# Attention: the row sums of two ticks of a pair are inverted together, in the later of the two ticks

## The chip, the cores and the metric

The kernel runs on one core of one Trainium2 chip. The metric is the device time of one execution in microseconds (us). The core has five engines with a queue of instructions each, which they work off in order: TensorE (PE in the profile, its weight loads PEld), VectorE (DVE), ScalarE (ACT), GpSimd (POOL) and SyncE (SP), which issues most of the transfers. An engine waits on semaphores that the others raise.

## The reference, cut to what matters

Three parts follow one another: an attention, a mixture of experts and a gated layer. The change lies in the attention.

```python
# q, k, v: (4, 8, 576, 64) = batch, heads, sequence, head width
scores = scale * np.matmul(q, k.transpose(0, 1, 3, 2))
mask = block_i >= block_j                  # blocks of 64 positions
scores = np.where(mask, scores, -1000000000.0)
scores = scores - np.max(scores, axis=-1, keepdims=True)
attn = np.exp(scores)
attn = attn / (np.sum(attn, axis=-1, keepdims=True) + 1e-09)
return np.matmul(attn, v).astype(np.float32)
```

Its output goes through eight experts of width 1024, weighted by a router that is normalised by rows and columns eight times, and then through a gated layer of width 1536.

## The kernel before

The attention works on 16 pairs of heads (two heads side by side on the 128 partitions). A pair's 576 query rows are nine chunks of 64, and chunk c needs the keys up to its own block, 64 (c+1) of them. A pair is cut into eight ticks u = 0 to 7 (`TICKS`): u=0 holds chunks 0 and 1, u=1 chunks 2 and 3, u=2 to u=5 hold chunks 4 to 7 one by one, and u=6 and u=7 are the two halves of chunk 8. One loop runs over all ticks of all pairs, and the work of a tick u is spread over later ticks:

- in its own tick `scores` (PE, lines 931 and 942, tile s) and `maxima` (DVE: the row maxima, line 954, and the bias of the exponential, line 963);
- one tick later `exps` (ACT, line 971: the exponential into the tile e of its chunk, and the row sums into tile sum);
- two ticks later `normalise`: DVE adds 1e-9 to the sums (line 990, for u=7 line 986) and inverts them (line 991, tile r), and POOL multiplies each chunk's e by its column of r (line 996). For u=6 it does nothing, since chunk 8 has its whole sum only with u=7;
- four ticks later `transposes`: PE turns the multiplied e (lines 1019 for u=0 and u=1, 1028 for the others, tile t), and ACT copies t to tile a (lines 1022 and 1029), which frees t;
- `values` (PE, line 1046, tile x) multiplies with v, and `take` (ACT, line 1061, tile xf) evacuates it.

The program's order is written out by hand: within a tick stand first the scores, then the transposes of four ticks ago, the additions and splits for the experts that are pending (lines 1079, 1088, 188, 190, 193), `normalise` of two ticks ago and the maxima, then the exponentials of the tick before. Between these parts the loop draws, at a fixed rate, pieces of the first two experts' matmuls (lines 537 and 600 on PE, with their evacuations and splits at 554 to 574, 754 and 758 on ACT and DVE), of the splitting of weights (178, 182, 303, 375), and the scaling of the next pairs' q and k (880, 895, 899, and PE's line 110, which spreads a maximum over the partitions). The tile t has one buffer, s three, x one.

The later parts, the experts from line 1293 on and the gated layer, start their own loops when the attention is over.

Of the kernel before, what the change touches and what calls it, by code (L numbers as in the profile page):

```python
# [30 lines left out]
def attention_moe_glu_kernel(  # L31
# [764 lines left out]
    TICKS = [((0, 0, CB), (1, 0, 2 * CB)), ((2, 0, 3 * CB), (3, 0, 4 * CB))]  # L796
    TICKS += [((c, 0, (c + 1) * CB),) for c in range(4, 8)]
    TICKS += [((8, 0, 288),), ((8, 288, 576),)]
    NTK = len(TICKS)
# [5 lines left out]
    def attention(actx):  # L805
# [172 lines left out]
                    )  # L978

        def normalise(p, u):  # L980
            if u == NTK - 2:
                return
            g = st[p]
            cs = slice(TICKS[u][0][0], TICKS[u][-1][0] + 1)
            if u == NTK - 1:
                nc.vector.tensor_scalar(
                    g["r"][:, cs], g["sum"][:, cs], g["sum"][:, NC : NC + 1], 1e-9, op0=ALU.add, op1=ALU.add
                )
            else:
                nc.vector.tensor_scalar_add(g["r"][:, cs], g["sum"][:, cs], 1e-9)  # L990
            nc.vector.reciprocal(g["r"][:, cs], g["r"][:, cs])  # L991
            for c in range(cs.start, cs.stop):
                n = (c + 1) * CB
                ne = 'PPPPPPPPP'[c]
                if ne == 'P':
                    nc.gpsimd.tensor_scalar(  # L996
                        et[c][:, :n], et[c][:, :n], g["r"][:, c : c + 1], 1.0, op0=ALU.mult, op1=ALU.mult
                    )
                elif ne == 'D':
                    nc.vector.tensor_scalar_mul(et[c][:, :n], et[c][:, :n], g["r"][:, c : c + 1])  # L1000
                else:
                    nc.scalar.activation(et[c][:, :n], et[c][:, :n], AF.Copy, scale=g["r"][:, c : c + 1])
# [157 lines left out]
        for tk in range(tot + NTK):  # L1160
            p, u = divmod(tk, NTK)
# [12 lines left out]
            if on(tk - 2):  # L1174
                normalise(*divmod(tk - 2, NTK))
# [578 lines left out]
```

## Time and profile before

| | us |
|---|---|
| median of three runs | 2089.74 (2084.0 to 2094.1) |
| span of the profiled execution | 2083.4 |
| attention in the profiled execution | about 10 to 372 |
| TensorE busy in the span | 1949.0 (94%) |
| VectorE busy in the span | 1620.1 (78%) |
| ScalarE busy | 1379.9 (66%) |
| GpSimd busy | 612.8 (29%) |

The profile is one execution; its span runs from the first to the last instruction, and its own time with what lies around the span is not told apart from the three above. The span is 0.6 us under the fastest of the three runs and 6.3 under the median. Busy shares are means over all stages; only those of the attention's own stretches say something of this change.

### The profile page before, as it was taken

What the parts mean: (1) busy time and instruction counts of PE and PEld (TensorE: products, weight loads), DVE (VectorE), ACT (ScalarE), POOL (GpSimd) and SP (SyncE); (2) the same over time, 40 slices, a digit from 0 to 9 for tenths busy, and PEclk for the clock granted to TensorE, in tenths of its full rate; (3) what the DMA queues carried; (4) which work ended last, traced back from release to release, by engine and by line L of the source; (5) the groups of instructions that cost most, each with busy time, mean ns of one, the idle gap of its engine ahead of it and who ended that gap; (6) DMA issues with size and microseconds to landing.
All of it is one profiled execution on the core that took longest, in us unless ns stands there. A gap on an engine that the chain in (4) does not pass through costs nothing.

```text
span 2083.4 us, 47251 instructions
## 1 busy us (share of the span) xinstructions
PE 1949.0 (94%) x18378; PEld 1672.9 (80%) x18378; DVE 1620.1 (78%) x3455; ACT 1379.9 (66%) x2940; POOL 612.8 (29%) x873
## 2 busy tenths in 40 slices
PE   6789899799999999999999999999999988999998
PEld 3457676698888888888888888888888877988887
DVE  7887765668787887978878788888887877666666
ACT  5665766348777777878777777777776566544442
POOL 4534444102333333333332333333332123000000
PEclk9889999999999999999999999999999999999999
DMA  5433331306687866878668786777877100301112
GB/s 155 112 96 105 84 105 49 122 22 122 120 172 155 172 136 125 178 150 171 132 132 179 149 178 134 153 157 144 180 148 168 37 11 1 87 21 37 47 42 52
DMA packets 168721, 236.41 MB, mean 113 GB/s; under 512 B 16432, under 2 KB 85680, under 8 KB 168496
## 3 DMA queue, kind: packets, MB, share of 16 engines
q0 software_dynamic: 66560, 107.37, 30.8%
q1 hardware_dynamic: 101936, 126.01, 19.9%
q8 instruction: 144, 2.36, 0.5%
q14 instruction: 81, 0.66, 0.1%
HBM read 90.98 MB, written 24.38 MB: 55 GB/s over the span
## 4 chain that ended last, share of the span: by engine, by line
PE 55%; DVE 15%; ACT 5%; DMA 3%; issue 3%; SPq 0%; POOL 0%; ACTq 0%; DVEq 0%
PE abc_m_b L537 11%; PE m_o_b L645 11%; PE m_o_ac L645 8%; PE abc_m_c L537 5%; PE abc_m_a L537 3%; PE abc_v_b L537 3%; PE abc_g_b L537 3%; PE m_go_b L645 3%; PE m_go_ac L645 2%; DVE m_t L704 2%; DVE m_h L193 2%; DMA wr<-in_w_dram 2%; PE abc_v_c L537 1%; DVE w L182 1%; PE abc_g_c L537 1%
## 5 line engine op out<-in xcount | busy, mean ns | idle before, releaser
L537 PEld LDWEIGHTS <-w 128*128 128x128 f16 x6720 | 609.8, 98 | 110.9 <-issue 45.7
L645 PEld LDWEIGHTS <-m_h 128*128 128x128 f16 x5292 | 514.0, 98 | 69.0 <-issue 10.5
L537 PE MATMUL abc_m_b<-xs,w 128*128 128x256 f16 (+1 forms) x3840 | 476.6, 264 | 31.9 <-DVE m_t L559 29.4
L1443 POOL DMA_DIRECT2D acc<-ev x351 | 305.4, 895 | 581.3 <-ACT ev L1447 367.4
L645 PE MATMUL m_o_b<-w,m_h 128*128 128x256 f16 x3024 | 403.5, 273 | 7.9 <-ACT ev L1447 7.7
L645 PE MATMUL m_o_ac<-w,m_h 128*128 128x256 f16 x2268 | 309.4, 273 | 0.4 <-ACT ev L1447 0.4
L537 PE MATMUL abc_m_c<-xs,w 128*128 128x256 f16 (+1 forms) x1920 | 230.7, 263 | 2.2 <-DVE m_h L758 1.6
L1447 ACT ACTIVATE ev<-m_o_b,pe 128x256 f32<-128x256 f32 x351 | 161.7, 476 | 64.0 <-PE m_o_b L645 52.8
L1447 ACT ACTIVATE ev<-m_o_ac,pe 128x256 f32<-128x256 f32 (+1 forms) x234 | 135.7, 580 | 47.8 <-PE m_o_ac L645 46.4
L178 ACT ACTIVATE w<-wr,ws 128x512 f16<-128x512 f32 x210 | 150.5, 723 | 12.7 <-DVE ws L163 10.3
L182 DVE SCALAR_TENSOR_TENSOR w<-wr,ws,w 128x512 f16<-128x512 f32 x210 | 155.5, 747 | 1.4 <-ACT w L178 1.4
L1431 POOL DMA_DIRECT2D acc<-ev_s x65 | 73.6, 1132 | 259.1 <-ACT ev_s L1427 259.1
L683 ACT CAST m_h<-m_t 128x512 f16<-128x512 f32 (+1 forms) x210 | 121.8, 580 | 41.2 <-DVE m_t L704 40.3
L676 ACT ACTIVATE m_h<-m_t 128x512 f16<-128x512 f32 (+1 forms) x210 | 121.8, 582 | 35.8 <-DVE m_t L574 24.9
L193 DVE TENSOR_TENSOR m_h<-m_t,m_h 128x512 f16<-128x512 f32 (+1 forms) x210 | 133.1, 635 | 8.7 <-ACT m_h L683 8.4
L680 DVE SCALAR_TENSOR_TENSOR m_h<-m_t,m_h 128x512 f16<-128x512 f32 (+1 forms) x210 | 132.2, 635 | 5.8 <-ACT m_h L676 5.6
L537 PEld LDWEIGHTS <-gg_w 128*128 128x128 f16 x1260 | 113.5, 98 | 22.2 <-issue 10.7
L996 POOL TENSOR_SCALAR e<-e,r 128x64 f32<-128x64 f32 (+2 forms) x144 | 78.1, 548 | 166.8 <-DVE r L991 111.9
L645 PEld LDWEIGHTS <-g_h 128*128 128x128 f16 x1134 | 111.0, 99 | 18.9 <-issue 5.4
L537 PEld LDWEIGHTS <-gv_w 128*128 128x128 f16 x1260 | 113.6, 98 | 13.2 <-issue 1.7
L537 PE MATMUL abc_m_a<-xs,w 128*128 128x256 f16 (+1 forms) x960 | 117.5, 262 | 0.0
L375 DVE TENSOR_REDUCE wmx<-wr 128x1 f32<-128x512 f32 x128 | 85.7, 679 | 15.0 <-DMA wr<-in_w_dram 14.9
(298 smaller groups left out, 3364.0 us busy)
## 6 DMA issues: line engine op xcount, KB each, us to landing
acc<-ev POOLq DMA_DIRECT2D x351, 256.0 KB, 4.3
wr<-in_w_dram SPq DMA_DIRECT2D x128, 256.0 KB, 4.8
acc<-ev_s POOLq DMA_DIRECT2D x52, 256.0 KB, 4.3
st<-hl SPq DMA_DIRECT2D x48, 144.0 KB, 3.6
raw_g<-in_w_gate_dram SPq DMA_DIRECT2D x12, 512.0 KB, 5.5
raw_v<-in_w_val_dram SPq DMA_DIRECT2D x12, 512.0 KB, 4.5
raw_o<-in_w_out_dram SPq DMA_DIRECT2D x12, 512.0 KB, 5.0
scr_g<-gg SPq DMA_DIRECT2D x21, 256.0 KB, 2.9
```

Source lines behind the costliest of these rows:

```text
L178: nc.scalar.activation(hi, src, AF.Copy, scale=s)
L182: nc.vector.scalar_tensor_tensor(lo, src, s, hi, op0=ALU.mult, op1=ALU.subtract)
L193: nc.vector.tensor_sub(lo, src, hi)
L375: nc.vector.tensor_reduce(g["mx"][:, k : k + 1], g["b"][k // 2][k % 2], axis=AX.XY, op=ALU.max, apply_absolute_value=True)
L537: nc.tensor.matmul(ps[:, f], W[o][:, sh, k, f * P : (f + 1) * P], xs[:, o, mh, k, c0 : c0 + n], start=x not in begun, stop=True, skip_grou ...
L645: nc.tensor.matmul(ps, h[o][:, sh, k, ii * P : (ii + 1) * P], W[o][:, mh, k], start=o in (X11, X12) and k == 0 and j == 0, stop=True, skip ...
L676: nc.scalar.activation(hi, src, AF.Relu)
L680: nc.vector.scalar_tensor_tensor(lo, src, 0.0, hi, op0=ALU.max, op1=ALU.subtract)
L683: nc.scalar.copy(hi, src)
L996: nc.gpsimd.tensor_scalar(et[c][:, :n], et[c][:, :n], g["r"][:, c : c + 1], 1.0, op0=ALU.mult, op1=ALU.mult)
L1443: nc.gpsimd.dma_start(acc[:, x], e, accum_op=ALU.add)
L1447: nc.scalar.activation(e[:, cols], ps, AF.Copy, scale=p)
```

## The change

`normalise` does nothing any more for u = 0, 2, 4 and 6, and for u = 1, 3 and 5 it takes the chunks of the tick before along with its own: DVE adds and inverts four columns at u=1 and two at u=3 and u=5, and POOL then multiplies all their chunks one after the other. u=7 is left as it was, and so are all other functions.

```diff
         def normalise(p, u):
-            if u == NTK - 2:
+            if u < NTK - 1 and u % 2 == 0:
                 return
             g = st[p]
-            cs = slice(TICKS[u][0][0], TICKS[u][-1][0] + 1)
+            cs = slice(TICKS[u - (u < NTK - 1)][0][0], TICKS[u][-1][0] + 1)
             if u == NTK - 1:
```

VectorE's queue in pair 9, before, from the maxima of u=1 (s_1) to those of u=4 (s_4); r_2807 is the pair's tile of inverses:

```order
496 L954 TENSOR_REDUCE negm_2804<-s_1_2853 128x1 x2
498 L990 TENSOR_SCALAR r_2807<-sum_2806 128x2
499 L991 RECIPROCAL r_2807<-r_2807 128x2
500 L954 TENSOR_REDUCE negm_2804<-s_2_2888 128x1
503 L758 SCALAR_TENSOR_TENSOR m_1_h_2915<-m_1_t_2768,m_1_h_2915 128x512
505 L843 TENSOR_REDUCE vmx_2579<-vs_1_2800 128x1
506 L990 TENSOR_SCALAR r_2807<-sum_2806 128x2
507 L991 RECIPROCAL r_2807<-r_2807 128x2
508 L954 TENSOR_REDUCE negm_2804<-s_3_2927 128x1
512 L990 TENSOR_SCALAR r_2807<-sum_2806 128x1
513 L991 RECIPROCAL r_2807<-r_2807 128x1
514 L954 TENSOR_REDUCE negm_2804<-s_4_2962 128x1
```

The same place of VectorE's queue in the changed kernel, where the pair's inverses are r_2753:

```order
442 L954 TENSOR_REDUCE negm_2750<-s_1_2799 128x1 x2
444 L954 TENSOR_REDUCE negm_2750<-s_2_2834 128x1
447 L758 SCALAR_TENSOR_TENSOR m_1_h_2857<-m_1_t_2713,m_1_h_2857 128x512
449 L843 TENSOR_REDUCE vmx_2527<-vs_1_2746 128x1
450 L990 TENSOR_SCALAR r_2753<-sum_2752 128x4
451 L991 RECIPROCAL r_2753<-r_2753 128x4
452 L954 TENSOR_REDUCE negm_2750<-s_3_2869 128x1
456 L954 TENSOR_REDUCE negm_2750<-s_4_2906 128x1
```

The two instructions for u=0 ahead of s_2 are gone, those ahead of s_3 now hold four columns, and those of u=2 ahead of s_4 have moved on to the place of u=3. Over the whole program VectorE has 96 instructions fewer, six in each of 16 pairs.

GpSimd's queue in pair 9, before, from the multiplication of chunk 4 (e_132, tick u=2) to that of chunk 7 (e_137, u=5); the rows at 1088, 188 and 1079 are pending additions and splits for the experts:

```order
222 L996 TENSOR_SCALAR e_132<-e_132,r_2807 128x320
223 L1088 TENSOR_TENSOR s_8_1_2999<-xf_8_1_2997 128x160
224 L188 TENSOR_SCALAR xs<-xf_8_1_2997 128x160
225 L996 TENSOR_SCALAR e_134<-e_134,r_2807 128x384
228 L1079 TENSOR_TENSOR xs<-xf_8_1_2997,xs 128x160
230 L996 TENSOR_SCALAR e_135<-e_135,r_2807 128x448
231 L1088 TENSOR_TENSOR xf_8_0_2739<-xf_8_0_2739,xf_9_0_3053 128x4x32
232 L996 TENSOR_SCALAR e_137<-e_137,r_2807 128x512
```

The same place of GpSimd's queue in the changed kernel:

```order
222 L1088 TENSOR_TENSOR s_8_1_2940<-xf_8_1_2938 128x160
223 L188 TENSOR_SCALAR xs<-xf_8_1_2938 128x160
224 L996 TENSOR_SCALAR e_132<-e_132,r_2753 128x320
225 L996 TENSOR_SCALAR e_134<-e_134,r_2753 128x384
228 L1079 TENSOR_TENSOR xs<-xf_8_1_2938,xs 128x160
230 L1088 TENSOR_TENSOR xf_8_0_2687<-xf_8_0_2687,xf_9_0_2995 128x4x32
231 L996 TENSOR_SCALAR e_135<-e_135,r_2753 128x448
232 L996 TENSOR_SCALAR e_137<-e_137,r_2753 128x512
```

The multiplications of chunks 4 and 6 now stand directly ahead of those of chunks 5 and 7, behind the pending work of the tick between. The queues of TensorE, ScalarE and SyncE hold the same instructions in the same order as before.

## Rows read from the trace of the kernel before

**Rows 1.** Busy time of each engine in four stretches of the attention.

```profile
core 0: us, PE busy (x) PEld busy (x) DVE busy (x) ACT busy (x) POOL busy (x), PEclk, DMA share, GB/s
10.00:100.00 90.00, 65.08 (x436) 32.69 (x436) 75.53 (x248) 55.23 (x160) 45.68 (x100) 0.85 0.41 121
100.00:160.00 60.00, 47.81 (x395) 32.90 (x396) 51.46 (x150) 40.73 (x102) 23.66 (x48) 0.89 0.37 99
160.00:280.00 120.00, 112.04 (x1032) 81.75 (x1031) 84.74 (x275) 76.05 (x204) 52.73 (x124) 0.99 0.35 98
280.00:372.00 92.00, 86.16 (x781) 62.44 (x779) 56.71 (x188) 59.66 (x160) 39.98 (x88) 0.96 0.24 67
```

**Rows 2.** Lines 990 and 991 on VectorE (ns min/median/max, first and last start).

```profile
L990 DVE TENSOR_SCALAR r<-sum x96: 138/148/263, 11.5 to 363.5; 128x1 f32<-128x1 f32 x64, 128x2 f32<-128x2 f32 x32
L991 DVE RECIPROCAL r<-r x112: 162/164/168, 11.7 to 369.8; 128x1 f32<-128x1 f32 x80, 128x2 f32<-128x2 f32 x32
```

**Rows 3.** Timeline of VectorE, pair 9: start us, us, instruction, [idle before <- releaser].

```profile
212.03 0.17 DVE L990 TENSOR_SCALAR r<-sum 128x2 f32<-128x2 f32 x1 [0.67 <-ACT e L971]
212.24 0.17 DVE L991 RECIPROCAL r<-r 128x2 f32<-128x2 f32 x1
212.32 0.47 DVE L954 TENSOR_REDUCE negm<-s 128x1 f32<-128x320 f32 x1
...
214.33 0.69 DVE L758 SCALAR_TENSOR_TENSOR m_h<-m_t,m_h 128x512 f16<-128x512 f32 x1 [0.70 <-ACT m_h L754]
...
216.59 0.17 DVE L991 RECIPROCAL r<-r 128x2 f32<-128x2 f32 x1
...
220.64 0.14 DVE L990 TENSOR_SCALAR r<-sum 128x1 f32<-128x1 f32 x1
```

**Rows 4.** Timeline of GpSimd, pair 9.

```profile
212.57 0.66 POOL L996 TENSOR_SCALAR e<-e,r 128x64 f32<-128x64 f32 x2 [1.23 <-DVE r L991]
216.95 0.88 POOL L996 TENSOR_SCALAR e<-e,r 128x192 f32<-128x192 f32 x2 [3.72 <-DVE r L991]
```

**Rows 5.** Timeline of TensorE, pair 9.

```profile
215.25 0.38 PE L1019 MATMUL t<-ident,e 128*128 128x128 f32 x2
...
224.71 0.44 PE L942 MATMUL s<-st,st 128*64 128x288 f16 x4 [1.56 <-ACT xf L1061]
...
228.12 0.70 PE L110 MATMUL qk_a<-qk_d,ones 128*128 128x256 f32 x2 [1.77 <-DVE r L990]
```

**Rows 6.** Timeline of ScalarE, pair 9.

```profile
218.37 0.66 ACT L971 ACTIVATE e<-s,bias,sc 128x384 f32<-128x384 f32 x1
218.92 0.20 ACT L971 ACTIVATION_READ_ACCUMULATOR e<-s,bias,sc 128x1 f32 x1
...
224.20 0.46 ACT L1061 ACTIVATE xf<-x,vs 128x256 f32<-128x256 f32 x1
```

**Rows 7.** Timeline of GpSimd, pairs 8 and 10.

```profile
196.49 0.88 POOL L996 TENSOR_SCALAR e<-e,r 128x192 f32<-128x192 f32 x2 [2.40 <-ACT a L1029]
...
238.85 0.88 POOL L996 TENSOR_SCALAR e<-e,r 128x192 f32<-128x192 f32 x2 [0.65 <-DVE r L991]
...
246.51 0.64 POOL L996 TENSOR_SCALAR e<-e,r 128x448 f32<-128x448 f32 x1
...
250.39 0.69 POOL L996 TENSOR_SCALAR e<-e,r 128x512 f32<-128x512 f32 x1 [2.95 <-DVE r L991]
```

**Rows 8.** Timeline of TensorE, pairs 8 and 10.

```profile
196.42 0.41 PE L1019 MATMUL t<-ident,e 128*128 128x128 f32 x2 [0.16 <-ACT a L1029]
...
239.03 0.38 PE L1019 MATMUL t<-ident,e 128*128 128x128 f32 x2
...
250.03 0.63 PE L1028 MATMUL t<-ident,e 128*128 128x128 f32 x4 [1.14 <-ACT a L1029]
```

**Rows 9.** Timeline of GpSimd, pair 0.

```profile
17.05 0.88 POOL L996 TENSOR_SCALAR e<-e,r 128x192 f32<-128x192 f32 x2 [4.28 <-DVE r L991]
```

**Rows 10.** Timeline of TensorE, pair 0.

```profile
12.86 0.44 PE L1019 MATMUL t<-ident,e 128*128 128x128 f32 x2
19.51 0.76 PE L110 MATMUL v_a<-v_d,ones 128*128 128x128 f32 x2 [6.21 <-DVE r L990]
```

## The prediction

> **What bounds the kernel now.** I read the stages first, since a mean over the whole span says nothing of an edit that touches only the attention. In the table of windows [rows 1] the reader is to see two regimes. From 10 to 160 us VectorE is the fullest engine (75.53 of 90 and 51.46 of 60 us, 84% and 86%), and TensorE has gaps (72% and 80%). From 160 to 372 us it is the other way round: TensorE is busy for 112.04 of 120 and 86.16 of 92 us (93% and 94%), VectorE for 71% and 62%. So in the first regime an instruction taken from VectorE may be worth its time, and in the second a wait put on TensorE is likely to cost most of its own.
>
> Then I read the timelines of single pairs, engine by engine, because the change moves an event (the moment at which a chunk's e is multiplied) and keeps all matmuls. The attention repeats itself about every four pairs (a batch; 12 pairs take the 280 us from about 92 to 372), so pairs 8 to 10 stand for the rest [rows 3 to 8].
>
> **What the change removes.** In each pair three pairs of instructions (990 and 991) go: 48 in all, with medians of 148 and 164 ns [rows 2]. On the queue such a pair holds the engine from its start to that of the next instruction: 212.32 - 212.03 = 0.29 us in pair 9 [rows 3]. 48 x 0.29 = 13.9 us of VectorE's time over the attention, 0.87 a pair. The reader is not to take that as the gain. In the second regime VectorE has slack of 29 to 38%, and the instruction that is freed often runs into another wait: in pair 9 the two instructions for u=0 are followed, two rows on, by line 758, which waited 0.70 us for ScalarE [rows 3]. Whatever comes off in front of it only lengthens that wait. There I take nothing. In the first regime seven pairs run (0 to 6): 7 x 0.87 = 6.1 us come off an engine at 84 to 86%. Bounds nothing and 6.1; I take 2.3, nearer to nothing, since VectorE is not full there either and waits are spread over all engines.
>
> The first wait also goes: at u=0 line 990 sat idle for 0.67 us until ScalarE's exponentials were done [rows 3]. The maxima of u=2 behind it can start that much sooner. In pair 9 this ends at the same line 758, so I price it at nothing.
>
> The Trainium skill (Perfetto Trace Analysis, Optimizing Scalar/DVE Operations) gives about 60 ns of engine time per VectorE instruction on SBUF, half of what a profile shows as its duration, and says that grouping helps if the engine is saturated. By that price the 96 instructions would be an estimate of 5.8 us instead of 13.9; the row of this kernel, a chained pair in 0.29 us, is what I go by.
>
> **What the change moves.** For u = 0, 2 and 4 the multiplication by r comes one tick later, while TensorE's transposes stay where they are, four ticks after the scores. Before, two ticks lay between; now only one. Nothing says that the engines keep step: TensorE runs ahead of VectorE. The new moment can be read from the trace. POOL's multiplication for u=1 began at 216.95 in pair 9, since it waited for line 991 [rows 4]. In the changed kernel the two chunks of u=0 go first there, and took 0.66 us [rows 4], so they are ready at 217.61. TensorE transposed them at 215.25 [rows 5]. It would have to wait 2.36 us. The same subtraction elsewhere:
>
> - pair 8, u=0: 196.49 + 0.66 against 196.42, 0.73 us [rows 4, 7, 8];
> - pair 10, u=0: 238.85 + 0.66 against 239.03, 0.48 us [rows 4, 7, 8];
> - pair 10, u=4: 250.39 + 0.64 (chunk 6) against 250.03, 1.00 us [rows 7, 8].
>
> At the other eight of the twelve places in pairs 8 to 11 the subtraction comes out the other way, and the transposes find their e ready. Sum for a period of four pairs: 4.57 us; for the three periods from 92 to 372 us 13.7 us.
>
> How much of a stall stays? I follow the one of 2.36 us. Behind the transposes TensorE's whole queue waits, and ScalarE waits for the copy of t and then for xf. Its exponential of u=3, at 218.37, comes at 220.73; its sum, done at 218.92 + 0.20, is done at 221.48 [rows 6]. Line 990 of u=3, which now carries u=2 as well, ran at 220.64 and would run at 221.5, 0.86 late [rows 3]: VectorE had been that far behind anyway. From there the lateness of 0.9 goes on through ScalarE's m_h to xf at 224.20 [rows 6], and the scores that waited 1.56 us for this xf begin at 225.6 instead of 224.71 [rows 5]. So of 2.36 us TensorE gets 1.5 back out of an idle time that it had already, and 0.9, two fifths, stay. With the same share for the others, 0.4 x 13.7 = 5.5 us stay. Bounds: nothing, if all the stalls find such idle time, and 13.7, if none does.
>
> The first four pairs are the program's start. In pair 0 the subtraction gives 17.05 + 0.66 - 12.86 = 4.85 us [rows 4, 9, 10], the largest of all, but TensorE's next instruction waited until 19.51 for VectorE anyway, 6.21 us [rows 10], so it costs nothing. Pairs 1 to 3 have places on both sides; there I take what stays of one period, 1.8 us, with bounds of nothing and 4.6, one period's whole stalls.
>
> POOL itself does the same multiplications in other groups; it is busy for 40 to 51% of these stages [rows 1], and nothing is priced for it. The pending additions that now stand ahead of chunks 4 and 6 come earlier, which VectorE may use; the memset of the next v stands behind one multiplication more, 0.6 us, with several ticks to spare.
>
> **Sum.** Stalls that stay, 5.5 in the three periods and 1.8 in the first four pairs, less 2.3 from VectorE: + 5.0 us, on the profiled 2083.4 us 2088.4. That execution's span lies 6.3 us under the median of the three runs; on the median the forecast is 2094.7 us. After the attention nothing changes, so that the difference is carried to the end as it is.
>
> **The rivals.**
>
> *The stalls stay whole* (slower). TensorE is at 93 and 94% in the second regime [rows 1]; if the idle times that took up 1.5 of 2.36 us in pair 9 move along with the stall, the cost is 13.7 + 4.6 = 18.3 us, less 2.3: + 16, 2105.7 us. For it: ScalarE copies t in order with its exponentials, so it is held up with TensorE. Against it: the waits of 1.56 and 1.77 us [rows 5] lie right behind the largest stall. The Trainium skill (Perfetto Trace Analysis, Optimizing Scalar/DVE Operations) speaks for this one: where VectorE is not saturated but makes other engines wait, it advises to break instructions up so that work is done sooner, and this change does the reverse.
>
> *VectorE's time comes through* (faster). Without the wait for the exponentials of u=0 (0.67 us in pair 9 [rows 3]) and with 0.29 us less per place, the joint inverses could come early enough for TensorE, and all of 13.9 us could reach the end: 13.9 less the stalls that stay in spite of it, say 1.8, is 12 us, 2077.6 us. It decides at the moment of line 991 of u=1: in pair 9 it would have to come 2.4 us sooner than 216.59 [rows 3]. Against it: the wait for ScalarE at 214.33 stands between.
>
> *The clock* (slower). The granted clock is 0.85 and 0.89 in the two stages in which TensorE has gaps, and 0.99 and 0.96 in the two in which it has hardly any [rows 1]. New gaps of 1 to 2.4 us could bring more stretches at the lower of the two levels. If the mean of the last 212 us fell by 0.05, their 198 us of busy TensorE would take some 10 us longer: with the forecast + 15, 2104.7 us.
>
> **How the numbers follow.** The forecast, between -10 and +10 us: 0.62. Stalls whole: 0.19. The clock: 0.07. VectorE's time comes through: 0.12. A difference of 0.5% is 10.4 us, about what a measurement of this kernel can tell from no change; so faster 0.12, same 0.62, slower 0.26. Range: up to 2107 it takes in both slower rivals' values, down to 2081 most of the forecast's own lower side (a gain of 9, VectorE's 6.1 us of the first regime and half of the rest, with no stall that stays); the faster rival lies outside.
>
> **What the profile of the changed kernel would show.** Lines 990 and 991 with 48 instructions each fewer, some 15 us less busy time on VectorE, and no wait of line 990 at u=0. TensorE waiting for POOL e (line 996) ahead of 1019, once or twice in four pairs and for up to 2.4 us, and ahead of 1028; shorter waits for ScalarE's xf and VectorE's qk_d behind these. The attention over at about 377 instead of 372 us, and the same times from there on. The prediction is wrong if these waits for POOL are there and the attention ends no later (absorbed whole), if they are not there at all (VectorE early), or if the end moves by more than 10 us (whole stalls, or a granted clock that fell).

## The result: slower by 0.57%, and the profile after

The changed kernel took 2099.46 us in the median of seven runs against 2087.31 us for the kernel before, ratio 1.0057, 95% interval 1.0045 to 1.007. That is 12 us more (9.4 to 14.6), where the prediction had 5. One of the seven, 2541.77 us at a granted clock of 0.748, was a disturbed run and is not in the ratio. The profiled execution has a span of 2096.9 us, 13.5 more than before.

First the windows of the attention, the same stretches as in [rows 1] and one more. The attention's last matmuls end at 391.2 us instead of 377.8. The 372 us that stand ahead for the kernel before, in the table, in [rows 1] and in the prediction, are some 6 us short of that end; and since its pair 4 begins at 83.7 us, its last twelve pairs take 294 us and not 280.

```profile
core 0: us, PE busy (x) PEld busy (x) DVE busy (x) ACT busy (x) POOL busy (x), PEclk, DMA share, GB/s
10.00:100.00 90.00, 66.58 (x384) 31.51 (x384) 71.35 (x213) 52.55 (x152) 42.27 (x95) 0.91 0.39 112
160.00:280.00 120.00, 108.23 (x935) 76.31 (x932) 79.22 (x228) 70.30 (x188) 49.12 (x110) 0.93 0.33 91
372.00:391.00 19.00, 18.27 (x170) 15.05 (x167) 5.82 (x18) 8.43 (x21) 6.58 (x14) 1.00 0.16 54
```

The reader is to see the stage from 160 to 280 us: TensorE was busy for 108.23 us there and got through 935 matmuls, where it had been busy for 112.04 us with 1032 [rows 1], at a granted clock of 0.93 instead of 0.99. It is not the same piece of the program in both, since everything is later; a comparison of like with like stands with the runs of some pairs below. The 0.91 of the first row does not show a faster clock than the 0.85 of [rows 1]: up to 28.5 us the view has 1.00 for the changed kernel, while the eight matmuls of line 1046 took 1.55 us there and 0.87 in the kernel before. The last row shows the end of the attention running where the kernel before, from 378 us, had begun its next part.

Who waited for POOL's multiplication is in the view of line 996 (us, times):

```profile
who waited for it (us, times):
  PEld t L1019: 21.1, 22
  PEld t L1028: 15.0, 13
  PE t L1019: 12.0, 8
  PE t L1028: 11.3, 8
```

These are the waits that the prediction forecast; the kernel before had 5.1 and 4.5 us of PEld in this view, and of PE 2.0 at line 1028 alone. Part of them replaces other waits, so they do not add up to a loss. Lines 990 and 991 answer to [rows 2]: 48 instructions each fewer, at about the same duration, though with two and four columns.

```profile
L990 DVE TENSOR_SCALAR r<-sum x48: 155/162/449, 15.8 to 376.8; 128x2 f32<-128x2 f32 x32, 128x4 f32<-128x4 f32 x16
L991 DVE RECIPROCAL r<-r x64: 162/166/178, 16.0 to 383.1; 128x2 f32<-128x2 f32 x32, 128x4 f32<-128x4 f32 x16, 128x1 f32<-128x1 f32 x16
```

Then pair 9, whose stall the prediction followed. VectorE, GpSimd, TensorE and ScalarE of the changed kernel, in this order of fences, each a timeline (start us, us, instruction, idle before):

```profile
222.74 0.69 DVE L758 SCALAR_TENSOR_TENSOR m_h<-m_t,m_h 128x512 f16<-128x512 f32 x1 [1.18 <-ACT m_h L754]
...
225.00 0.18 DVE L991 RECIPROCAL r<-r 128x4 f32<-128x4 f32 x1
...
231.55 0.30 DVE L990 TENSOR_SCALAR r<-sum 128x2 f32<-128x2 f32 x1 [2.82 <-ACT e L971]
```

```profile
225.35 2.08 POOL L996 TENSOR_SCALAR e<-e,r 128x64 f32<-128x64 f32 x4 [5.25 <-DVE r L991]
```

```profile
225.72 0.67 PE L1019 MATMUL t<-ident,e 128*128 128x128 f32 x2 [1.83 <-POOL e L996]
226.32 3.96 PE L1046 MATMUL x<-a,v 128*64 128x320 f32 x20
...
235.87 0.44 PE L942 MATMUL s<-st,st 128*64 128x288 f16 x4 [0.27 <-ACT xf L1061]
...
239.27 0.70 PE L110 MATMUL qk_a<-qk_d,ones 128*128 128x256 f32 x2 [1.77 <-DVE qk_d L103]
```

```profile
230.33 0.53 ACT L1061 ACTIVATE xf<-x,vs 128x320 f32<-128x320 f32 x1 [3.48 <-PE x L1046]
```

Line 758 now waits 1.18 instead of 0.70 us, as forecast: what came off in front of it lengthened its wait. TensorE waits 1.83 us for the four multiplications' first two, and the later wait for xf has shrunk from 1.56 [rows 5] to 0.27 us, while the one for qk_d, which was to shrink too, is 1.77 us as before. What the prediction did not have are the rows between: the two transposes took 0.67 us instead of 0.38 [rows 5], and the 20 matmuls of line 1046 right behind them 3.96 us. The row of the kernel before for the same 20, and then the same place in the run below that has the change in pairs 4 to 15 alone:

```profile
215.56 2.28 PE L1046 MATMUL x<-a,v 128*64 128x320 f32 x20
```

```profile
222.29 0.67 PE L1020 MATMUL t<-ident,e 128*128 128x128 f32 x2 [1.83 <-POOL e L997]
222.89 2.28 PE L1047 MATMUL x<-a,v 128*64 128x320 f32 x20
```

With the same wait of 1.83 us the 20 matmuls took 2.28 us there (that kernel's lines stand one further down). So the transposes are longer in both, but the slow matmuls behind the wait do not come every time.

### The profile page after: what moved, and what is told of

It reads as the page before. It is cut to its first block, busy times and chain, and to the rows that moved or that the text cites. A ratio compares the mean times of both kernels' runs of the same rounds, so it can differ in the third digit from the quotient of the medians.

```text
span 2096.9 us, 47134 instructions
## 1 busy us (share of the span) xinstructions
PE 1959.4 (93%) x18378; PEld 1676.3 (80%) x18378; DVE 1613.3 (77%) x3359; ACT 1378.7 (66%) x2940; POOL 613.2 (29%) x873
## 3 DMA queue, kind: packets, MB, share of 16 engines
q8 instruction: 144, 2.36, 0.5%
## 4 chain that ended last, share of the span: by engine, by line
PE 54%; DVE 16%; ACT 4%; DMA 4%; issue 3%; SPq 0%; POOL 0%; DVEq 0%; ACTq 0%
PE abc_m_b L537 11%; PE m_o_b L645 11%; PE m_o_ac L645 8%; PE abc_m_c L537 5%; PE abc_m_a L537 3%; PE abc_v_b L537 3%; PE abc_g_b L537 3%; PE m_go_b L645 3%; PE m_go_ac L645 2%; DVE m_t L704 2%; DVE m_h L193 2%; DMA wr<-in_w_dram 2%; DVE w L182 1%; PE abc_v_c L537 1%; PE abc_g_c L537 1%
## 5 line engine op out<-in xcount | busy, mean ns | idle before, releaser
L645 PEld LDWEIGHTS <-m_h 128*128 128x128 f16 x5292 | 514.0, 98 | 70.2 <-issue 11.7
L600 PEld LDWEIGHTS <-m_h 128*128 128x128 f16 x864 | 83.7, 99 | 16.9 <-issue 6.9
```

Of the source, the lines that this page charges most:

```text
L600: nc.tensor.matmul(p[:, c * TB : (c + 1) * TB], h[t, r][:, sh, k, ii * P : (ii + 1) * P], W[r, c][:, mh, k], start=c == 0 and j == 0, stop ...
L645: nc.tensor.matmul(ps, h[o][:, sh, k, ii * P : (ii + 1) * P], W[o][:, mh, k], start=o in (X11, X12) and k == 0 and j == 0, stop=True, skip ...
```

## The experiments

Each was timed in five rounds beside the kernel before on the same chip; the ratio is to that.

**The lateness without the grouping.** Every tick keeps its own instructions for the inverses, but those of the even ticks are issued at the place of the odd ones.

```diff
             if on(tk - 2):
-                normalise(*divmod(tk - 2, NTK))
+                pn, un = divmod(tk - 2, NTK)
+                if un % 2:
+                    for w in (un - 1, un) if un < NTK - 1 else (un,):
+                        normalise(pn, w)
```

> The lateness without the grouping: the sums of every tick are inverted by instructions of their own, as before (no VectorE instruction is saved), but those of u = 0, 2 and 4 only at the place of u = 1, 3 and 5. Theory 1 (TensorE waits for the e that is multiplied a tick later): as slow as the change or a little slower, + 12 to + 16 us on before, ratio 1.006 to 1.008, with waits of TensorE for POOL e at lines 1019 and 1028 as in the changed kernel. Rival (the grouped inverses themselves cost: a wait for the later sums, four columns in one instruction): as before, within 4 us, ratio 0.998 to 1.002. If the saved VectorE time is worth much, this one is slower than the change by its worth, up to 13.9 us.

Measured: 2102.45 us, ratio 1.0072 (1.0055 to 1.009), + 15 us. The lateness alone makes the whole loss; the grouping by itself takes none of it. Against the change it is 3 us slower, which may be what the saved VectorE instructions are worth there, but the intervals overlap.

**The saving without the lateness.** Line 990 is left out up to u=5, and the sums are inverted directly, in their own tick. The addition of 1e-9 is what it leaves out.

```diff
-            else:
-                nc.vector.tensor_scalar_add(g["r"][:, cs], g["sum"][:, cs], 1e-9)
-            nc.vector.reciprocal(g["r"][:, cs], g["r"][:, cs])
+            src = g["r"] if u == NTK - 1 else g["sum"]
+            nc.vector.reciprocal(g["r"][:, cs], src[:, cs])
```

> The saving without the lateness: line 990, the addition of 1e-9 to the sums, is left out for u = 0 to 5 and the sums (1 or more, so that the addition changes nothing in fp32) are inverted directly; every inverse stays in its own tick. 96 VectorE instructions fewer, as many as in the change. Theory 1 (the saving is worth little since VectorE is not the bound in most of the attention): 0 to 5 us faster than before, ratio 0.9975 to 1.000. Rival (VectorE's time comes through): 10 to 18 us faster, ratio 0.991 to 0.995.

Measured: 2077.9 us, ratio 0.9968 (0.9957 to 0.9979), 6.7 us faster, between the two expectations. 96 VectorE instructions fewer are worth something if nothing comes later for it. Each inverse also comes one instruction sooner here, and that part is not told apart. This version beats both kernels.

**One place of the change at a time.** First u=0 with u=1 alone, then u=2 with 3 and u=4 with 5 alone, shown as edits of the changed kernel.

```diff
-            if u < NTK - 1 and u % 2 == 0:
+            if u in (0, NTK - 2):
...
-            cs = slice(TICKS[u - (u < NTK - 1)][0][0], TICKS[u][-1][0] + 1)
+            cs = slice(TICKS[u - (u == 1)][0][0], TICKS[u][-1][0] + 1)
```

> One place of the change alone: u = 0 is inverted with u = 1, all other ticks as before. Theory 1: the waits at line 1019 (pairs 5, 8, 9, 12, 13, and pair 3) come, those at line 1028 do not; + 5 to + 9 us, ratio 1.002 to 1.0045. Rival (what costs is TensorE's clock, which falls after some gap wherever it is): no share that goes with the waits, anything from 0 to + 12 us, with the time at the lower clock between 160 and 372 us as the only thing that grew.

```diff
-            if u < NTK - 1 and u % 2 == 0:
+            if u in (2, 4, NTK - 2):
...
-            cs = slice(TICKS[u - (u < NTK - 1)][0][0], TICKS[u][-1][0] + 1)
+            cs = slice(TICKS[u - (u in (3, 5))][0][0], TICKS[u][-1][0] + 1)
```

> The other places alone: u = 2 with u = 3 and u = 4 with u = 5, while u = 0 and u = 1 are inverted apart as before. Theory 1: waits at line 1028 in pairs 1, 3, 4, 6, 10 and 14 only, + 3 to + 7 us, ratio 1.0015 to 1.0035; with the run that groups u = 0 and 1 alone it adds up to the + 12 us of the change. Rival (clock): the two do not add up.

Measured: 2095.18 us, ratio 1.0044 (1.0029 to 1.0059), + 9.2 us, and 2089.17 us, ratio 1.0015 (1.0006 to 1.0024), + 3.1 us. Together 12.3 us: the places add up to the change, three quarters of it at u=0. The intervals are some 3 and 2 us to either side, and the rival of these two runs, the clock, expected that they would not add up.

**Some pairs at a time.** The change in pair 0 alone, in pairs 0 to 3, and in pairs 4 to 15.

```diff
-            if u == NTK - 2:
+            joint = p == 0
+            if u == NTK - 2 or joint and u < NTK - 1 and u % 2 == 0:
...
-            cs = slice(TICKS[u][0][0], TICKS[u][-1][0] + 1)
+            cs = slice(TICKS[u - (joint and u < NTK - 1)][0][0], TICKS[u][-1][0] + 1)
```

> The joint inversion in pair 0 alone, all other pairs as before. The prediction priced pair 0 at nothing, since TensorE waits there for VectorE's spread of the maximum of v anyway: ratio 0.999 to 1.001. Rival (the clock: in the changed kernel's trace TensorE waits 3.5 us for POOL e in pair 0, its matmuls run at half rate until 28.8 instead of 24.2 us, and pair 2 begins 2.6 us later): + 1.5 to + 3 us, ratio 1.0007 to 1.0015.

In the other two `joint` is `p < 4` and `p >= 4`.

> The joint inversion in pairs 0 to 3 alone. The prediction's terms for them: 1.8 us of stalls that stay less about half of VectorE's 2.3, so + 1 us, ratio 0.9995 to 1.001. Rival (these pairs carry what the traces' marks show, pair 4 beginning 4.4 us later): + 3 to + 6 us, ratio 1.0015 to 1.003, and the runs of these four pairs and of the other twelve add up to the change's + 12 us.

> The joint inversion in pairs 4 to 15 alone, before them as in the kernel before. The prediction's terms: 5.5 us of stalls that stay less about half of 2.3, + 4 us, ratio 1.0015 to 1.0025. Rival (every stall stays or is given back as a slower clock): + 8 to + 14 us, ratio 1.004 to 1.0065.

Measured: ratio 1.0001 (0.9989 to 1.0013); 1.0013 (1.0002 to 1.0024), + 2.7 us; 1.0053 (1.004 to 1.0067), + 11 us. Pair 0 costs nothing, within some 2.5 us. The twelve later pairs carry the loss: 11 us (8 to 14) where the prediction's terms came to 4, and inside the range of that run's rival.

The last of these runs can be laid beside the kernel before from one pair to the next, since both begin pair 4 at 83.7 us. Windows between the first maxima of pairs 4, 8 and 12 and the end of the attention, kernel before and then pairs 4 to 15 joint:

```profile
83.67:186.01 102.34, 85.15 (x716) 58.70 (x716) 80.61 (x249) 66.15 (x170) 43.07 (x97) 0.87 0.37 100
186.01:277.03 91.02, 84.32 (x775) 60.66 (x776) 66.35 (x215) 59.88 (x160) 39.85 (x90) 0.98 0.36 101
277.03:377.85 100.82, 94.24 (x853) 68.62 (x854) 59.19 (x194) 62.75 (x168) 40.16 (x88) 0.97 0.24 66
sum 294.18, PE 263.71 PEld 187.99 DVE 206.15 ACT 188.78 POOL 123.08; mean PE 87.90 PEld 62.66 DVE 68.72 ACT 62.93 POOL 41.03
```

```profile
83.69:190.32 106.63, 87.01 (x716) 58.88 (x716) 78.78 (x224) 65.77 (x170) 43.43 (x97) 0.88 0.35 96
190.32:285.22 94.90, 86.32 (x775) 61.24 (x776) 65.11 (x191) 59.73 (x160) 40.79 (x90) 0.96 0.34 96
285.22:388.24 103.02, 94.97 (x853) 68.64 (x854) 57.76 (x170) 62.48 (x168) 41.01 (x88) 0.97 0.23 65
sum 304.55, PE 268.30 PEld 188.76 DVE 201.66 ACT 187.97 POOL 125.23; mean PE 89.43 PEld 62.92 DVE 67.22 ACT 62.66 POOL 41.74
```

The counts behind x are the same matmuls stage by stage. The attention is 10.4 us longer (304.55 - 294.18). TensorE's idle time grew by 5.8 us (36.25 - 30.47) and its busy time by 4.6 (268.30 - 263.71).

How far can one execution be trusted for this? The runs of pair 0 and of pairs 0 to 3 have pairs 4 to 15 as in the kernel before, and the changed kernel has them all joint. The sums of the three windows between the same marks, in this order:

```profile
sum 288.93, PE 258.96 PEld 185.43 DVE 205.91 ACT 187.89 POOL 122.52; mean PE 86.32 PEld 61.81 DVE 68.64 ACT 62.63 POOL 40.84
sum 291.70, PE 260.25 PEld 185.72 DVE 205.97 ACT 187.81 POOL 123.62; mean PE 86.75 PEld 61.91 DVE 68.66 ACT 62.60 POOL 41.21
sum 303.13, PE 266.77 PEld 187.78 DVE 202.03 ACT 187.81 POOL 124.68; mean PE 88.92 PEld 62.59 DVE 67.34 ACT 62.60 POOL 41.56
```

The idle time is 30.0 to 31.5 us in the three traces without the change in these pairs and 36.3 to 36.4 in the two with it: that growth is clear. The busy time is 259.0 to 263.7 us without it and 266.8 to 268.3 with it: it grew too, but by anything from 3 to 9 us, since the same code differs by 4.8 us from one execution to another.

What TensorE waited for ahead of the transposes in these pairs, kernel before and then pairs 4 to 15 joint (us in total, times, longest):

```profile
PE t L1028 <- ACT a L1029: 3.4, 3, 1.1
PE t L1028 <- POOL e L996: 0.7, 1, 0.7
PE t L1019 <- ACT a L1029: 0.3, 2, 0.2
```

```profile
PE t L1029 <- POOL e L997: 8.7, 5, 2.2
PE t L1020 <- POOL e L997: 6.8, 6, 2.1
```

So 15.5 us of waits stand where 4.4 stood, 11.1 more, at eleven places.

**Work in the waits.** To tell the second of these apart from the first, the change was given multiplications of constants in ten of its waits, 66 in all, which the kernel does not need.

```diff
             t = ps_t.tile([P, 4, P], F32, tag="t", name=f"t_{p}_{u}")
+            for _ in range({(0, 0): 12, (1, 4): 6, (3, 0): 7, (4, 2): 6, (5, 0): 6, (6, 4): 6, (9, 0): 6, (10, 4): 6, (13, 0): 4, (14, 4): 7}.get((p, u), 0)):
+                nc.tensor.matmul(t[:, 0], ones, ident, start=True, stop=True)
```

> The change, with multiplications of constants (128x128, fp32, into the tile t that is overwritten right after) put ahead of the transposes at ten of the places where TensorE waits for POOL e in the changed kernel's trace (pairs 0, 3, 5, 9 and 13 at u=0, 4 at u=2, 1, 6, 10 and 14 at u=4), 66 in all, as many as fit into each wait. They are work that the kernel does not need. Theory 2 (a good part of the loss is TensorE's clock: matmuls right after a wait take up to twice their time): the waits shrink but the e comes when it did, the matmuls behind run at their full rate, and the kernel is 4 to 9 us faster than the change, ratio to before 1.001 to 1.004. Theory 1 alone (the waits themselves are the loss): not faster than the change, ratio 1.005 to 1.008.

Measured: 2092.03 us, ratio 1.0033 (1.0019 to 1.0046), some 5 us less than the change's 1.0057 although TensorE has more to do. The granted clock of its executions averages 0.988, that of the change's 0.982 and of the kernel before 0.983. So the work in the waits raised the clock above that of the kernel before, and the 5 us need not be what the change had lost. One place shows how the clock comes in, u=4 of pair 10. First the changed kernel, TensorE's timeline and then the windows around it:

```profile
262.20 0.66 PE L1028 MATMUL t<-ident,e 128*128 128x128 f32 x4 [1.98 <-POOL e L996]
262.70 0.82 PE L537 MATMUL abc_m_b<-xs,w 128*128 128x256 f16 x6
264.77 0.96 PE L942 MATMUL s<-st,st 128*64 128x192 f16 x8 [1.26 <-ACT e L971]
265.66 1.46 PE L600 MATMUL abc<-w_(0, 0)_786,m_h 128*128 128x256 f16 x6
```

```profile
255.00:264.00 9.00, 6.54 (x63) 4.69 (x61) 6.94 (x21) 5.54 (x14) 4.37 (x10) 1.00 0.44 115
264.00:267.60 3.60, 2.83 (x18) 1.89 (x18) 2.83 (x11) 1.30 (x5) 2.00 (x5) 0.53 0.00 0
```

The same place with work in the wait:

```profile
253.17 1.60 PE L1015 MATMUL t<-ident,ones 128*128 128x128 f32 x12 [0.81 <-ACT a L1031]
254.61 0.60 PE L1030 MATMUL t<-ident,e 128*128 128x128 f32 x4
255.04 0.82 PE L537 MATMUL abc_m_b<-xs,w 128*128 128x256 f16 x6
257.12 0.57 PE L942 MATMUL s<-st,st 128*64 128x192 f16 x8 [1.26 <-ACT e L971]
257.63 0.83 PE L600 MATMUL abc<-w_(0, 0)_804,m_h 128*128 128x256 f16 x6
```

The wait of 1.26 us for ScalarE stands in both, and also stood in the kernel before, where a wait of 1.14 us preceded it [rows 8]. With the wait at the transposes lengthened to 1.98 us, the granted clock fell to 0.53 and the matmuls behind took 0.96 and 1.46 us; with work in it, 0.57 and 0.83. The fall does not follow each such wait: in pairs 4 to 15 the changed kernel has seven waits of 1.1 us or more at the transposes, and the granted clock of the next 8 us was under 1.00 behind three of them (pairs 6, 9 and 10); in the run of pairs 4 to 15 alone it was so behind three of seven as well (pairs 6, 10 and 14).

The same idea on the kernel before, meant for two of its own waits, gave nothing. But its second edit missed its place: "w10" is the spread at 88.99 us, which waits 1.26 us, and not the one of the second expert's that waits 4.42 us at 134.59.

```diff
         n = g["n"]
+        for _ in range({"v0": 14, "w10": 10}.get(g["name"], 0)):
+            nc.tensor.matmul(bank[:, :P], ones, ident, start=True, stop=True)
         g["row"] = bank[:, : n * P].rearrange("p (n q) -> p n q", n=n)
```

> The kernel before, with the same kind of unneeded multiplications ahead of the spread of a maximum at two of its own longest waits (14 ahead of that of v in pair 0, where TensorE idles 6.2 us, and 10 ahead of that of the second expert's first weights, 4.5 us). Theory 2: matmuls after these two waits no longer run at half rate (3.7 and 3.5 us over their usual times in the trace of before), 2 to 7 us faster, ratio 0.9965 to 0.999. Theory 1 alone: the same as before, ratio 0.999 to 1.002.

Measured: 2084.53 us, ratio 1.000 (0.9987 to 1.0013), at an average clock of 0.985. The number is theory 1's, but the run does not decide against theory 2. The next matmuls behind the first place, in the kernel before and then in this run, and after them the second place, again in both:

```profile
20.20 1.97 PE L931 MATMUL s<-k,q 64*64 64x512 f32 x4
```

```profile
19.35 1.07 PE L933 MATMUL s<-k,q 64*64 64x512 f32 x4
```

```profile
88.99 0.76 PE L110 MATMUL w_a<-w_d,ones 128*128 128x128 f32 x2 [1.26 <-DVE w_d L103]
```

```profile
86.60 4.22 PE L110 MATMUL w_a<-ident,ones 128*128 128x128 f32 x20 [0.84 <-ACT e L973]
...
132.94 0.80 PE L112 MATMUL w_a<-w_d,ones 128*128 128x128 f32 x2 [4.10 <-DVE w_d L103]
```

Behind the filled wait of v's spread the same four matmuls took 1.07 instead of 1.97 us, and pair 1 began at 26.4 instead of 27.9 us, as theory 2 has it. The ten at the second place took 4.22 us where a wait of 1.26 us had been, and the long wait it was meant for is still there, unfilled.

**The transposes moved after the late e.** With them at the end of their tick, and the same move on the kernel before as the control:

```diff
             out1 = None
-            if on(tk - 4):
+            if on(tk - 4) and tk % 2:
                 out1 = transposes(*divmod(tk - 4, NTK))
...
+            if on(tk - 4) and tk % 2 == 0:
+                transposes(*divmod(tk - 4, NTK))()
             if on(tk - 1):
                 exps(*divmod(tk - 1, NTK))
```

> The change, with the transposes of u = 0, 2 and 4 (and their copies out of t) moved from the first third to the end of their tick, so that TensorE does a piece of the experts, and for u = 0 the values of the pair before, ahead of them. Theory 1 (the waits of TensorE for the late e are the first cause of all of the loss): the waits for POOL e go, and what is left is the saved VectorE time: 0 to 7 us faster than before, ratio 0.9965 to 1.000. Rival (the joint inverses delay something else too, such as ScalarE's exponentials): still 4 to 12 us slower, ratio 1.002 to 1.006.

> Only the later transposes of u = 0, 2 and 4 on the kernel before, nothing joint: what the move of the transposes costs by itself. Theory 1: within 4 us of before, ratio 0.998 to 1.002, since the transposes of u = 0 to 4 have most of a tick to spare. If it is much slower, the run of the change with later transposes must be read against this one.

Measured: 2090.98 us, ratio 1.0025 (1.0012 to 1.0038) with the change, and 2090.86 us, ratio 1.0026 (1.0014 to 1.0037), without it. Both expectations were missed: the move alone costs 5 us, and why was not followed, and with the change it is 5 us slower than the kernel before, inside the rival's range. Beside that control, though, the change costs nothing any more. Nor does it give anything: the 96 instructions saved do not show. The waits of TensorE for POOL e did not all go. Of the change's 12.0 us at line 1019 one wait of 3.8 is left, and of its 11.3 us at line 1028 there are 9.0; the control has 0.7 at 1028:

```profile
PE t L1028 <- POOL e L996: 9.0, 8, 1.8
PE t L1019 <- POOL e L996: 3.8, 1, 3.8
```

So the saving and what is left of the waits may balance there; that was not taken apart, and the run supports the cause only in part.

## Why the prediction came out as it did

**The sign and its cause were right, the size was less than half.** It forecast + 5 us; measured were 12, beyond the 10 us up to which it gave its forecast a chance of 0.62, and among the slower outcomes, to which it gave 0.26. By its own sign of being wrong, too, the end of the attention was to move by no more than 10 us, and it moved by 13.3 (377.8 to 391.2). The cause it named, the e that comes a tick later to transposes that do not move, is shown by the run of the lateness alone (+ 15 us). The transposes' move agrees with it, less firmly, since the move itself cost 5 us.

**The stalls were right.** In pair 9 the trace has 1.83 us of wait where 2.36 were worked out, and 0.27 instead of 1.56 us in the wait behind, so that 1.3 us came back of the 1.5 forecast. Over pairs 4 to 15 the waits at the transposes grew by 11.1 us where 13.7 were worked out, and TensorE's idle time by 5.8 us where 5.5 were to stay. That the second agrees so well is partly luck: half of the stalls stayed instead of two fifths, of a smaller sum, and the 5.8 us have what VectorE saved in them, which the prediction took off separately. Pair 0, priced at nothing, cost nothing, and pairs 0 to 3 together cost 2.7 us (0.4 to 5.0) where the terms came to 1.

**The step that failed** is the sum's assumption that a stall costs only its own idle time: "so of 2.36 us TensorE gets 1.5 back out of an idle time that it had already, and 0.9, two fifths, stay". TensorE's busy time for the same matmuls was taken to stay as it was, and in these twelve pairs it grew by 4.6 us in the two traces laid side by side. If their matmuls are matched one by one, those that ran at the full level of the clock in both took 2.9 us more, nearly all of it in the transposes that wait, as the 0.67 instead of 0.38 us of pair 9; what lengthens them was not taken apart. The other 1.7 us lie where one trace or both were at the lower level.

**The clock** stood among the rivals, with a chance of 0.07 and a price of some 10 us. It has a part, as pair 10 shows, but how large a part is not settled. Among the 35 executions of the kernel before beside which the filled kernel was timed, 0.001 of the mean clock goes with some 1.0 us; by that estimate the 0.006 that the filled kernel has above the change are 6 us, all of its gain, and the 0.0015 that the change lies under the kernel before are 1.5 of its 12 us. The run of u=0 alone cost 9.2 us at the mean clock of the kernel before (0.983). The means miss the first 28.5 us of the changed kernel, where the view has 1.00 although its matmuls took longer.

**VectorE's term**, - 2.3 us, was of the right order where it stands: the change is 3 us faster than the same lateness without the saving, though not clear of noise. By itself, with no lateness, the saving of as many instructions gave 6.7 us, not the 13.9 of their queue time. The profile was to show some 15 us less busy time on VectorE. The rows of lines 990 and 991 did fall by 13.2 us (33.3 to 20.1), but rows of VectorE overlap, as at 212.24 us in [rows 3], and its busy time, which counts an overlap once, fell by only 6.8 us (1620.1 to 1613.3), and by 13.7 in the run without the addition (to 1606.4); why these two differ was not followed. The Trainium skill's price (Perfetto Trace Analysis, Optimizing Scalar/DVE Operations), an estimate of 5.8 us, lies nearer to the 6.7 us.

**The rival of whole stalls**, + 16 us, and that of VectorE's time coming through, - 12 us, did not come; the first was nearer than the forecast in size, though by another way: half of the stalls did come back out of other idle time, and part of the loss is busy time. The measured 0.57% is just over the bound of 0.5% beyond which the forecast counted it as slower. In the reason for the range, VectorE's 6.1 us and half of the rest make 10.0 and not 9; nothing else hangs on it.

## What to carry to other kernels

Before instructions are joined to save an engine's queue time, subtract, place by place, the moment at which its reader stands ready in the trace from the moment at which the joint one's result can be there; where the reader is the engine that sets the time, a difference above nothing is a new wait. Follow each new wait to the next old one behind it, since part of it comes back there, and do not take the engine's busy time as fixed: here it grew by almost as much as its idle time. If the saving is what is wanted, look for an instruction that can go without making anything later: here the addition ahead of the inverse.

## What had not been expected of the hardware

Two transposes that waited 1.83 us took 0.67 us where they took 0.38 without the wait, with the clock at its full level. The 20 matmuls behind them took 3.96 us in one kernel and 2.28 in another with the same wait. Lengthening one of two neighbouring waits from 1.14 to 1.98 us went with a granted clock of 0.53 in the next 3.6 us, and such falls followed three of seven waits in each of two traces. Unneeded multiplications put into ten such waits raised the mean clock from 0.982 to 0.988 and made the kernel some 5 us faster. In a wait of 6.2 us they let the next matmuls run in 1.07 instead of 1.97 us; whether the whole kernel gains by that alone was not measured.
